# A new order list for all engines, and a maximum of routing codes in three steps instead of one reduction

## The chip, the cores and the metric

The kernel runs on one core of a Trainium2 chip. The core has five engines that run their instruction lists side by side and meet at semaphores: TensorE (PE; its weight loads are shown as PEld), VectorE (DVE), ScalarE (ACT), GpSimdE (POOL) and SyncE (SP), which issues all transfers here. The metric is the device time of one execution, in microseconds, as a median of several runs.

## The reference

Two branches share a layer norm of x (2048 tokens, 576 values); their sum is added to x.

```python
xn = layernorm(x)                                  # S = 2048, D = 576
y_A = irfft2(rfft2(xn) * (w_r + 1j * w_i))         # over tokens and values
q = einsum("nd,dhc->nhc", xn, w_q)                 # 32 heads, 2 x 128
s1 = einsum("nhd,ed->nhe", q[..., :128], k1)       # 8 keys
s2 = einsum("nhd,ed->nhe", q[..., 128:], k2)
e = argmax(s1) * 8 + argmax(s2)                    # one expert of 64 per head
act = gelu(einsum("nd,nhd->nh", xn, u[e]))
y_B = einsum("nh,nhd->nd", act, v[e])              # softmax over one choice is 1
out = x + y_A + y_B
```

## The kernel before

All data stays on the chip after one load of x (`XN`). The program is written in stages, each a function that names its instructions; a planner collects them as operations and issues them in an order of its own.

Branch A goes through matrix products. For each of 16 groups `t` of 128 tokens, `ln` computes mean and spread, and `folds` folds a row of 576 values at its middle: `e`, two halves of 289 (in the trace `t<-XN`, since its slots are called `t1`), then `F`, four quarters (`A<-t` in the trace, slots `A2`). `Rs` is the Fourier matrix of 128 points scaled by the row's spread. `dft128` multiplies (`Rs,A` and `Rs,yl` on TensorE), and each result is split into a rounded part, copied out, and a residual, subtracted by VectorE (`AB<-banks`, `ABL<-banks`). For 16 groups `g` of frequencies follow `d_fwd` (transform along the values, `c,AB` and `c,ABL`), `s_fwd` (the rest of the token transform, 64 x 64 tiles, two groups packed), `s_mul` (the product with the filter `Wt`, two VectorE operations `t<-banks,wx,Wt` a group, combined on GpSimdE as `y` and split as `yh`), and `s_inv` (64-row tiles, `s,yh` and `s,yl`). At the end, per token group, `d_inv` goes back along the values and `fin` adds both branches and writes out.

Branch B never forms the queries. `fold_part` multiplies the differences of the keys (`KP`) into the query weights (32 tiles `w` of 576 KB, five buffers, 32-column tiles of TensorE). Four sums come out; ScalarE copies each to `MT`, VectorE centres it with `mm_`, it is transposed and split into `MU` and `MUL`. `scores` multiplies x transposed (`xT`, made from `xf` by `x_t`) with them, for 256 tokens a round, in eight rounds: 448 score differences a token, 64 choices (`m`) of 7 (`e`), and 64 dot products with `u`. The maximum over the seven is `mx`; `eq` marks where it is reached (0 or 1, two bytes); `eq` times a code per choice (`wt`) goes into the second part of `wk` (slots `w`, so `w<-banks,mx` and `w<-w,wt` in the trace). `route` takes the maximum over the seven codes (`MT<-w`, 128x128 from 896), zeroes it where the first key wins (`MT<-mx,MT`), and forms a table of 8 x 32 codes; `combine` turns it into weights, which `fin` multiplies with `v`.

What sets the order: an operation that may run on more than one engine is written with `FG`, `FV`, `FP` or `FA`, and the letter of `PICK` at its place decides (v VectorE, a ScalarE, g GpSimdE). The list `RANK` has a number per operation. `_Plan.forward` walks time from modelled costs: at each step the engine that is free first takes, among the operations that are ready, the one with the lowest rank, within limits on how many PSUM tiles of a kind are open (`LIMIT`). The order found so is issued; each engine executes its part strictly in that order, SyncE its transfers too. PSUM banks are chosen at the same time.

Of the kernel before, what the change touches and what calls it, by code (L numbers as in the profile page):

```python
# [32 lines left out]
def _consts():  # L33
# [300 lines left out]
class _Plan:  # L334
# [113 lines left out]
    def forward(self, prio):  # L448
# [24 lines left out]
        def choice(e):  # L473

            now, soon, cand = free[e], INF, []
            for i in wait[e]:
                if pre[i]:
                    continue
# [801 lines left out]
```

## Time and profile before

| | |
|---|---|
| median of 3 runs | 226.01 us (225.72 to 227.08) |
| the profiled execution | 225.55 us |
| its span, first to last instruction | 223.8 us |
| busy: TensorE / VectorE / GpSimdE / ScalarE | 195.3 / 198.6 / 152.5 / 128.1 us |
| loaded and written | 38.33 MB, 4.72 MB |
| granted TensorE clock | 1.00 throughout |

A busy time is the time in which an engine has an instruction running. Almost every instruction carries the line number L585, where the planner issues it, so the rows are told apart by the names of their output and inputs (`out<-in`) and by their shapes. A busy TensorE is not one at its peak, since its products overlap in the pipe. [...]

### The profile page before, as it was taken

What the parts mean: (1) busy time and instruction counts of PE and PEld (TensorE: products, weight loads), DVE (VectorE), ACT (ScalarE), POOL (GpSimd) and SP (SyncE); (2) the same over time, 40 slices, a digit from 0 to 9 for tenths busy, and PEclk for the clock granted to TensorE, in tenths of its full rate; (3) what the DMA queues carried; (4) which work ended last, traced back from release to release, by engine and by line L of the source; (5) the groups of instructions that cost most, each with busy time, mean ns of one, the idle gap of its engine ahead of it and who ended that gap; (6) DMA issues with size and microseconds to landing.
All of it is one profiled execution on the core that took longest, in us unless ns stands there. A gap on an engine that the chain in (4) does not pass through costs nothing.

```text
span 223.8 us, 5983 instructions
## 1 busy us (share of the span) xinstructions
PE 195.3 (87%) x2287; PEld 135.7 (61%) x2287; DVE 198.6 (89%) x442; ACT 128.1 (57%) x270; POOL 152.5 (68%) x222
## 2 busy tenths in 40 slices
PE   0069788999999899699899899999979989999993
PEld 0068456677767666565455545655565678787872
DVE  2999999788978997883899999999999999999973
ACT  2278976777767974948475566391545342243330
POOL 3999899991079953745564865893677376689590
PEclk9999999999999999999999999999999999999999
DMA  6999999999999994333525331201100001432415
GB/s 209 421 418 410 364 347 372 408 404 350 343 397 409 400 406 156 113 90 106 151 98 155 89 113 38 61 2 37 35 3 0 3 1 56 160 127 87 158 53 211
DMA packets 14571, 43.41 MB, mean 194 GB/s; under 512 B 1872, under 2 KB 4688, under 8 KB 14160
## 3 DMA queue, kind: packets, MB, share of 16 engines
q1 hardware_dynamic: 14544, 43.05, 52.4%
q8 instruction: 17, 0.28, 0.5%
q14 instruction: 10, 0.08, 0.1%
HBM read 38.33 MB, written 4.72 MB: 192 GB/s over the span
## 4 chain that ended last, share of the span: by engine, by line
PE 41%; DVE 30%; POOL 10%; ACT 6%; issue 6%; DMA 6%; POOLq 0%; ACTq 0%; DVEq 0%
PE banks L585 41%; DVE t L585 7%; DVE w L585 4%; DVE MT L585 4%; DVE AB L585 4%; POOL y L585 3%; DVE A L585 3%; DMA xf<-in_xT_dram 2%; DVE st L585 2%; POOL xT L585 2%; DMA XN<-in_x_dram 2%; DMA w<-in_wq_dram 2%; POOL t L585 1%; DVE ABL L585 1%; POOL A L585 1%
## 5 line engine op out<-in xcount | busy, mean ns | idle before, releaser
L585 PE MATMUL banks<-MU,xT 128*128 128x512 f16 x192 | 46.2, 379 | 0.9 <-DVE w L585 0.7
L585 POOL TENSOR_TENSOR A<-t 128x145 f32<-128x145 f32 (+3 forms) x54 | 36.3, 690 | 5.1 <-DVE t L585 2.8
L585 POOL TENSOR_TENSOR xT<-xf,xT 64x128 f16<-64x128 f32 (+1 forms) x31 | 25.4, 820 | 20.8 <-ACT xT L585 19.4
L585 PEld LDWEIGHTS <-xT 128*128 128x128 f16 x224 | 21.0, 98 | 23.1 <-issue 1.4
L585 PE MATMUL banks<-c,AB 128*128 128x145 f16 (+1 forms) x384 | 34.7, 228 | 0.1
L585 PEld LDWEIGHTS <-AB 128*128 128x128 f16 x384 | 31.5, 122 | 4.6 <-issue 2.9
L585 POOL TENSOR_TENSOR y<-t,t 128x289 f32<-128x289 f32 x30 | 23.0, 788 | 11.2 <-DVE t L585 10.7
L585 POOL TENSOR_TENSOR yh<-y,yh 128x578 f16<-128x578 f32 x16 | 20.4, 1285 | 6.8 <-ACT yh L585 5.7
L585 PE MATMUL banks<-Rs,yl 128*99 128x128 f32 x64 | 11.1, 313 | 15.8 <-DVE Rs L585 13.3
L585 DVE SCALAR_TENSOR_TENSOR t<-banks,wx,Wt 128x578 f32<-128x578 f32 x32 | 24.2, 810 | 0.6 <-issue 0.3
L585 POOL TENSOR_TENSOR t<-XN 128x289 f32<-128x289 f32 x28 | 21.8, 792 | 3.3 <-DMA XN<-in_x_dram 2.9
L585 ACT ACTIVATE yh<-banks,sc 128x580 f32<-128x580 f32 x16 | 11.9, 747 | 20.9 <-PE banks L585 13.5
L585 DVE TENSOR_TENSOR AB<-banks,AB 128x512 f16<-128x512 f32 x32 | 21.6, 677 | 0.9 <-ACT AB L585 0.8
L585 PE MATMUL banks<-A,c 128*128 128x288 f32 x64 | 21.4, 416 | 0.2 <-POOL A L585 0.2
L585 PEld LDWEIGHTS banks<-Rs,yl 128*99 128x99 f32 x64 | 8.6, 187 | 20.4 <-ACT Rs L585 15.6
L585 PE MATMUL banks<-w,KP 128*32 128x288 f32 x256 | 20.9, 416 | 0.0
L585 ACT ACTIVATE AB<-banks 128x512 f16<-128x512 f32 x29 | 16.9, 589 | 6.6 <-PE banks L585 6.5
L585 PE MATMUL banks<-c,ABL 99*128 99x289 f16 (+1 forms) x64 | 18.6, 291 | 2.0 <-DVE t L585 1.6
L585 PE MATMUL banks<-Rs,A 128*128 128x128 f32 x128 | 18.4, 297 | 0.0
L585 DVE TENSOR_REDUCE MT<-w 128x128 bf16<-128x896 bf16 (+1 forms) x16 | 18.2, 1143 | 0.1
L585 PEld LDWEIGHTS banks<-Rs,A 128*128 128x128 f32 x128 | 17.0, 210 | 1.4 <-DVE A L585 0.5
L585 ACT ACTIVATE xf<-xf,bx 128x640 f32<-128x640 f32 x15 | 12.3, 823 | 8.0 <-DMA xf<-in_xT_dram 8.0
(141 smaller groups left out, 431.7 us busy)
## 6 DMA issues: line engine op xcount, KB each, us to landing
w<-in_wq_dram SPq DMA_DIRECT2D x32, 576.0 KB, 6.6
xf<-in_xT_dram SPq DMA_DIRECT2D x16, 320.0 KB, 4.4
Wt<-in_W_dram SPq DMA_DIRECT2D x8, 578.0 KB, 5.9
out_dram<-XN SPq DMA_DIRECT2D x14, 288.0 KB, 2.1
XN<-in_x_dram SPq DMA_DIRECT2D x3, 1154.0 KB, 9.1
s<-in_s_dram SPq DMA_DIRECT2D x16, 192.0 KB, 4.0
XN<-in_x_dram SPq DMA_DIRECT2D x2, 577.0 KB, 4.6
c<-in_c_dram SPq DMA_DIRECT2D x1, 868.5 KB, 8.2
```

The lines of the kernel that those rows point to most:

```text
L585: fn(*[x.place() if isinstance(x, _Ps) else x for x in args], **{k: x.place() if isinstance(x, _Ps) else x for k, x in kw.items()})
```

## The change

It has three parts. First, `RANK` becomes the order itself: operations are sorted by it, and a function `follow` replaces `forward` and only works out start times and PSUM banks along that list; `prepare` and `LIMIT` go. The list is a new one. `PICK` is new, too, and the four small `KP` differences get a letter. The model's cost of a GpSimdE operation with a reversed input is changed, which alters nothing but modelled times and, through them, which PSUM bank a tile gets. Second, the marks and codes of a round lie choice-major (`e` ahead of `m`), so that the comparison reads the scores in PSUM in steps of seven values. Third, the maximum over seven codes is taken in three tensor-tensor steps.

```diff
-        eq = wk[:, 0:896].rearrange("p (t m e) -> p t m e", t=2, e=7)
-        V.tensor_tensor(eq, sv, mx.unsqueeze(3).to_broadcast([128, 2, 64, 7]), op=OP.is_equal)
+        eq = wk[:, 0:896].rearrange("p (t e m) -> p t e m", t=2, e=7)
+        V.tensor_tensor(eq, sv.rearrange("p t m e -> p t e m"), mx.unsqueeze(2).to_broadcast([128, 2, 7, 64]),
+                        op=OP.is_equal)
...
-        wv = wk[:, 896:1792].rearrange("p (m e) -> p m e", e=7)
+        wv = wk[:, 896:1792].rearrange("p (t n) -> p t n", t=2)
...
-        V.tensor_reduce(v0, wv, axis=AX, op=OP.max)
+        V.tensor_tensor(wv[:, :, 192:384], wv[:, :, 0:192], wv[:, :, 192:384], op=OP.max)
+        V.tensor_tensor(wv[:, :, 320:448], wv[:, :, 192:320], wv[:, :, 320:448], op=OP.max)
+        V.tensor_tensor(v0.rearrange("p (t m) -> p t m", t=2), wv[:, :, 320:384], wv[:, :, 384:448], op=OP.max)
...
-    V.tensor_copy(wt.rearrange("p (m e) -> p m e", e=7), mk[:, 20:27].unsqueeze(1).to_broadcast([128, 64, 7]))
+    V.tensor_copy(wt.rearrange("p (e m) -> p e m", e=7), mk[:, 20:27].unsqueeze(2).to_broadcast([128, 7, 64]))
...
-        G.tensor_tensor(KP[:, :, s, 8 * s:8 * s + 7], kT[:, :, 1:8],
-                        kT[:, :, 0:1].to_broadcast([128, 2, 7]), op=OP.subtract)
+        FG.tt(KP[:, :, s, 8 * s:8 * s + 7], kT[:, :, 1:8], kT[:, :, 0:1].to_broadcast([128, 2, 7]), OP.subtract)
...
 RANK = (
-    48, 77, 55, 80, 93, 89, 58, 63, 129, 70, 96, 118, 150, 100, 154, 40, 236, 73, 102, 111, 108, 44, 194,
...
+    3, 19, 14, 16, 76, 107, 2, 75, 51, 39, 143, 181, 0, 6, 15, 22, 13, 25, 1, 12, 40, 237, 5, 4, 8, 9, 7,
...
-        _, order, slot, start = self.forward([-r for r in RANK])
+        order = sorted(range(len(ops)), key=lambda i: RANK[i])
+        _, slot, start = self.follow(order)
```

Three places of the new order follow. On SyncE's queue, around the last tiles of query weights (`w<-in_wq`; `Wt` are filter tiles, `xf` tiles of x transposed, `s` matrices of the token transform), there stood before:

```order
L585 DMA s_0_114<-in_s_dram 128x768
L585 DMA s_1_115<-in_s_dram 128x768
L585 DMA w_118<-in_wq_dram 128x1152
L585 DMA w_122<-in_wq_dram 128x1152
L585 DMA w_119<-in_wq_dram 128x1152
L585 DMA xf_125<-in_xT_dram 128x640
L585 DMA s_3_117<-in_s_dram 128x768
L585 DMA xf_123<-in_xT_dram 128x640
```

and now, at the last tiles of query weights:

```order
L493 DMA s_0_114<-in_s_dram 128x768
L493 DMA w_118<-in_wq_dram 128x1152
L493 DMA w_119<-in_wq_dram 128x1152
L493 DMA w_122<-in_wq_dram 128x1152
L493 DMA s_2_116<-in_s_dram 128x768
L493 DMA s_3_117<-in_s_dram 128x768
L493 DMA Wt_112<-in_W_dram 128x1156
L493 DMA xf_124<-in_xT_dram 128x640
L493 DMA xf_123<-in_xT_dram 128x640
```

Ahead of the last query tile the queue now holds three filter tiles and four `xf` tiles, before five and six; in the whole queue the numbers are the same.

On ScalarE, at the copy of the last folded sum (`MT,mm__94<-banks`), before:

```order
L585 ACTIVATE ABL<-banks 99x2x128
L585 ACTIVATE xf_123<-xf_123,bx 128x640
L585 ACTIVATE xf_125<-xf_125,bx 128x640
L585 ACTIVATE MT,mm__94<-banks 128x576
L585 ACTIVATE A_1_99<-banks 128x578
```

and now:

```order
L493 ACTIVATE AB<-banks 128x4x128
L493 ACTIVATE ABL<-banks 99x2x128
L493 ACTIVATE xT_93<-xf_123 128x640
L493 ACTIVATE MT,mm__94<-banks 128x576
L493 ACTIVATE A_1_99<-banks 128x578
```

The two scalings of freshly loaded `xf` tiles are no longer right ahead of the copy.

On VectorE, in the second round of scores (`mx_131`; `w_121` holds its marks and codes), before:

```order
L585 TENSOR_REDUCE mx_131<-banks 128x128
L585 TENSOR_TENSOR xT_93<-xf_123,xT_93 128x512
L585 TENSOR_TENSOR w_121<-banks,mx_131 128x896
L585 TENSOR_TENSOR AB<-banks,AB 128x4x128
L585 TENSOR_TENSOR ABL<-banks,ABL 33x2x128
L585 TENSOR_TENSOR w_121<-w_121,wt 128x896
L585 TENSOR_TENSOR MT<-MT,fm 128x128
L585 TENSOR_REDUCE MT<-w_121 128x128
```

and now:

```order
L493 TENSOR_REDUCE mx_131<-banks 128x128
L493 TENSOR_TENSOR w_121<-banks,mx_131 128x896
L493 TENSOR_TENSOR w_121<-w_121,wt 128x896
L493 SCALAR_TENSOR_TENSOR t_0_96<-banks,wx,Wt_113 128x578
L493 SCALAR_TENSOR_TENSOR t_1_107<-banks,wx,Wt_113 128x578
L493 TENSOR_TENSOR w_121<-w_121 128x2x192
L493 TENSOR_TENSOR w_121<-w_121 128x2x128
L493 TENSOR_TENSOR y_134<-t_1_107,t_0_96 128x289
L493 SCALAR_TENSOR_TENSOR t_1_97<-banks,wx,Wt_113 128x578
L493 SCALAR_TENSOR_TENSOR t_0_106<-banks,wx,Wt_113 128x578
L493 TENSOR_TENSOR A_0_98<-banks,A_0_98 128x578
L493 TENSOR_TENSOR ABL<-banks,ABL 33x2x128
```

The one reduction has become three tensor-tensor maxima (the third stands two rows further on), with filter products in between.

More of the change, by code (lines that the diff above doesn't have):

```diff
@@ L138 @@
 RANK = (
[66 rows of a table removed]
[66 rows of a table added]
 )
 PICK = (
[L207 to L211 removed]
+    "ggggvgggvagggvvaaavgggaaaagvvvaaaagggvaaaavvvgaaaavgvgvaaavgggaaaagvggaaaagvggaaaagvggaaaaggvgaaaavv"
+    "ggaaaagvvvaaaagvggagaavgggagaaaaaggaaaavgavaaggaaggaaggaaggaavgaagggaaaaggagaggagaaaggagaaaavgaaggaa"
+    "ggaggagagaaaggagaaaaggaaggaaggagaagagaaaggagaaaaggaavgaagvaggagavaaagvagaaaaggaavgaaggagaagagaaaggag"
+    "aaaaggaaggaaggagaavavaaaggagaaaaggagaagggaaaggagaaaggagaggvaaaaaagaagvgagvvagvgagggagvgagggagggagvva"
+    "gvgagggagggagggaggvagggagggaggg"
 )
[L213 removed]
 WORDS = {"mxr": 1, "mxd": 4, "st": 48, "Rs": 128, "t1": 578, "t2": 578, "A2": 578, "y": 578,
@@ L261 @@
 class _Op:
-    __slots__ = ("shape", "tiles", "eng", "calls", "cost", "lat", "deps", "succ", "stage", "pre", "port",
-                 "held", "opens", "after", "bk", "label", "flex")
+    __slots__ = ("shape", "tiles", "eng", "calls", "cost", "lat", "deps", "stage", "port", "bk", "flex")
 def _mask(ap):
@@ L362, in cost @@
             if m == "tensor_tensor":
-                return (60 + 2.05 * n if size_of(out.dtype) == 4 else 175 + 1.92 * n), 75.0
+                rev = any(d[0] < 0 for i in ins for d in i.ap[1:])
+                return (60 + 2.05 * n + (110 if n == 289 and rev else 42 * rev) if size_of(out.dtype) == 4
+                        else 175 + 1.92 * n + (80 if n == 128 else 0)), 75.0
             return ((45 if n > 16 else 280) + (3.02 if ptr else 1.15) * n if ins else 60 + 1.15 * n), 75.0
@@ L399, in add @@
             op.flex = None
-            op.eng, op.calls, op.cost, op.lat, op.deps, op.succ, op.stage = eng, [], c, lat, set(), [], self.stage
+            op.eng, op.calls, op.cost, op.lat, op.deps, op.stage = eng, [], c, lat, set(), self.stage
             op.tiles, op.port, op.bk = tiles, port, []
@@ L430, in latency @@
         return o.lat + (80.0 if o.eng == "vector" and s.eng == "gpsimd" else 0.0)
-    def prepare(self):
-        ops = self.ops
-        for i, o in enumerate(ops):
-            o.pre = set()
-            for j in o.deps:
-                ops[j].succ.append(i)
-        after = [0] * len(ops)
-        for i in reversed(range(len(ops))):
-            for k in ops[i].succ:
-                after[i] |= after[k] | 1 << k
-        for v in {v for o in ops for v in o.tiles if v.kind != "f"}:
-            i = min(v.users)
-            ops[i].pre |= {j for u in v.users for j in ops[u].deps
-                           if j != i and not after[i] >> j & 1 and ops[j].eng != "sync"}
@@ L448, in forward @@
-    def forward(self, prio):
-        ops = self.ops
-        free = {e.name: 0.0 for e in self.engines}
-        need = [len(o.deps) for o in ops]
-        ready = [0.0] * len(ops)
-        pre = [len(o.pre) for o in ops]
-        left = {v: len(v.users) for v in self.tiles}
-        end, slot = dict.fromkeys(left, 0.0), {}
-        wait = {e: [i for i, o in enumerate(ops) if o.eng == e and not o.deps] for e in free}
-        free_at = [0.0] * 8
-        def banks(tiles):
-            f, when, first = list(free_at), 0.0, []
-            for v in tiles:
-                n = v.banks
-                t = {k: max(f[k:k + n]) for k in range(0, 9 - n, n)}
-                lo = min(t.values())
-                k = max((k for k in t if t[k] == lo), key=lambda k: (f[k ^ 1] if n == 1 else -k))
-                f[k:k + n] = [INF] * n
-                when = max(when, lo)
-                first.append(k)
-            return when, first
[L473 to L478, printed above, removed]
-                o, t = ops[i], ready[i]
-                for b in o.bk:
-                    for x, u in seen.get(b, ()):
-                        if x != e and u > t:
-                            t = u
-                if o.opens:
-                    new = [v for v in o.opens if v not in slot]
-                    if new:
-                        k = new[0].kind
-                        tb = banks(new)[0]
-                        if used[k] + len(new) > LIMIT[k] or tb == INF:
-                            continue
-                        t = max(t, tb)
-                soon = min(soon, t)
-                cand.append((t, i))
-            if not cand:
-                return None
-            t0 = max(now, soon)
-            return t0, e, max((prio[i], -i) for t, i in cand if t <= t0)
-        used, port, cold, seen = {k: 0 for k in LIMIT}, 0.0, 4500.0, {}
-        order, start = [], [0.0] * len(ops)
-        shape = None
-        best, stale, full = dict.fromkeys(free), set(free), [0.0, 0.0]
-        while len(order) < len(ops):
-            for e in best:
-                if e in stale:
-                    best[e] = choice(e)
-            t0, e, (_, i) = min((b for b in best.values() if b), key=lambda b: b[0])
-            i = -i
-            wait[e].remove(i)
-            o, cost = ops[i], ops[i].cost
@@ new lines, in follow @@
+    def follow(self, order):
+        ops, free = self.ops, {e.name: 0.0 for e in self.engines}
+        end, late, seen, slot, cur = {}, {}, {}, {}, [None] * 8
+        port, cold, shape, full = 0.0, 4500.0, None, [0.0, 0.0]
+        start = [0.0] * len(ops)
+        for i in order:
+            o, e, cost = ops[i], ops[i].eng, ops[i].cost
+            t = free[e]
+            for j in o.deps:
+                t = max(t, end[j] + self.latency(ops[j], o) + late.get(j, 0.0))
+            for b in o.bk:
+                for x, u in seen.get(b, ()):
+                    if x != e:
+                        t = max(t, u)
+            new = [v for v in sorted(o.tiles, key=lambda v: v.order) if v not in slot] if e == "tensor" else []
+            if new:
+                f = [max(end.get(j, INF) + ops[j].lat for j in v.users) if v else 0.0 for v in cur]
+                for v in new:
+                    n = v.banks
+                    w = {k: max(f[k:k + n]) for k in range(0, 9 - n, n)}
+                    lo = min(w.values())
+                    k = max((k for k in w if w[k] == lo), key=lambda k: (f[k ^ 1] if n == 1 else -k))
+                    slot[v] = k
+                    f[k:k + n], cur[k:k + n] = [INF] * n, [v] * n
+                    t = max(t, lo)
@@ L511, in forward @@
             if e == "tensor":
                 if shape is not None and o.shape[0] != shape:
-                    t0 = max(t0, free[e] + CHANGE)
+                    t = max(t, free[e] + CHANGE)
                 shape = o.shape[1]
-                gap = t0 - free[e]
+                gap = t - free[e]
                 if gap > 2000:
-                    cold = t0 + 3600
-                elif t0 < cold and gap > 600:
+                    cold = t + 3600
+                elif t < cold and gap > 600:
@@ L520, in forward @@
                     cold += gap
-                if t0 < cold:
-                    cost += min(cost, (cold - t0) / 2)
-            elif o.port and port > t0:
-                t0 = port
-            order.append(i)
-            start[i] = t0
-            stale = {e}
-            for k in o.held:
-                pre[k] -= 1
-                if not pre[k]:
-                    stale.add(ops[k].eng)
-            free[e] = t0 + cost
+                if t < cold:
+                    cost += min(cost, (cold - t) / 2)
+            elif o.port:
+                t = max(t, port)
@@ L533, in forward @@
+            start[i], free[e], end[i] = t, t + cost, t + cost
             if o.port:
@@ L536, in forward @@
                 seen.setdefault(b, []).append((e, free[e] + o.lat))
-                stale |= {"vector", "scalar"}
-            if o.opens:
-                new = [v for v in o.opens if v not in slot]
-                for v, k in zip(new, banks(new)[1]):
-                    slot[v] = k
-                    free_at[k:k + v.banks] = [INF] * v.banks
-                    used[v.kind] += 1
-                stale.add("tensor")
-            for v in o.tiles:
-                left[v] -= 1
-                end[v] = max(end[v], free[e] + o.lat)
-                if not left[v]:
-                    free_at[slot[v]:slot[v] + v.banks] = [end[v]] * v.banks
-                    used[v.kind] -= 1
-                    stale.add("tensor")
-            lag = 0.0
             if e == "sync":
-                if t0 > full[1]:
-                    full[0] = t0
+                if t > full[1]:
+                    full[0] = t
                 full[1] = free[e] + 300
-                lag = 2600.0 if t0 - full[0] > 1500 else 0.0
-            for k, lat in o.after:
-                ready[k] = max(ready[k], free[e] + lat + lag)
-                need[k] -= 1
-                if not need[k]:
-                    wait[ops[k].eng].append(k)
-                    stale.add(ops[k].eng)
-        return max(free.values()), order, slot, start
+                late[i] = 2600.0 if t - full[0] > 1500 else 0.0
+        return max(free.values()), slot, start
     def issue(self):
-        self.prepare()
         ops = self.ops
-        self.tiles = sorted({v for o in ops for v in o.tiles}, key=lambda v: v.order)
-        for o in ops:
-            o.held = []
-            o.opens = sorted(o.tiles, key=lambda v: v.order) if o.eng == "tensor" else []
-            o.after = [(k, self.latency(o, ops[k])) for k in o.succ]
-        for i, o in enumerate(ops):
-            for j in o.pre:
-                ops[j].held.append(i)
-        _, order, slot, start = self.forward([-r for r in RANK])
+        order = sorted(range(len(ops)), key=lambda i: RANK[i])
+        _, slot, start = self.follow(order)
         self.order = [(start[i], i) for i in order]
```

6 lines of the change are left out of this document (removed), and 130 rows, old and new, of the table RANK.

## Prediction

> **What bounds the kernel now.** I read the busy times of the page first, then the busy time per stage, cutting the span at VectorE's first and last maximum over scores (`mx`), then single instructions.
>
> ```profile
> PE 195.3 (87%) x2287; PEld 135.7 (61%) x2287; DVE 198.6 (89%) x442; ACT 128.1 (57%) x270; POOL 152.5 (68%) x222
> L585 DVE TENSOR_REDUCE mx<-banks x8: 1074/1076/1092, 104.4 to 178.6; 128x128 f32<-128x896 f32 x8
> 0.00:104.40 104.40, 84.75 (x1069) 60.72 (x1070) 86.49 (x224) 73.11 (x163) 72.95 (x122) 1.00 0.87 328
> 104.40:178.60 74.20, 69.83 (x871) 41.97 (x870) 72.73 (x140) 40.61 (x84) 48.86 (x59) 1.00 0.20 59
> 178.60:223.80 45.20, 40.71 (x351) 33.01 (x349) 39.37 (x80) 14.35 (x24) 30.73 (x43) 1.00 0.28 106
> 0.00:89.90 89.90, 71.80 (x916) 52.36 (x916) 76.36 (x201) 62.41 (x145) 65.68 (x113) 1.00 0.95 362
> 177.20:220.30 43.10, 41.99 (x362) 34.14 (x362) 40.25 (x82) 14.66 (x25) 31.71 (x43) 1.00 0.26 99
> ```
>
> Columns after the stretch and its length: busy us of PE, PEld, DVE, ACT, POOL, then clock, DMA share, GB/s. Three stages have three limits. Before 104.4 us VectorE is busy 86.5 us and idle 17.9, of which 13.5 lie before 89.9 (89.9 - 76.4). In the middle it is busy 72.7 of 74.2 us: the limit, with TensorE (69.8) close behind. At the end TensorE is busy 42.0 of 43.1 us.
>
> The first stage hangs on memory and on a chain behind it:
>
> ```profile
> 0.73 3.89 DMA XN<-in_x_dram
> 50.00:60.00 10.00, 9.79 (x106) 7.72 (x106) 8.78 (x30) 7.39 (x18) 1.06 (x3) 1.00 0.98 350
> 70.00:80.00 10.00, 9.43 (x159) 6.07 (x156) 9.85 (x21) 8.69 (x18) 9.24 (x11) 1.00 1.03 404
> 78.95 0.33 SPq L585 DMA_DIRECT2D w<-in_wq_dram  x1
> 87.29 0.69 PE L585 MATMUL banks<-w,KP 128*32 128x288 f32 x8
> 87.56 1.55 ACT L585 ACTIVATE xf<-xf,bx 128x640 f32<-128x640 f32 x2 [3.13 <-DMA xf<-in_xT_dram]
> 89.01 0.63 ACT L585 ACTIVATE MT<-banks 128x576 f32<-128x576 f32 x1
> 89.77 0.15 DVE L585 TENSOR_SCALAR mm__94<-mm__94 128x1 f32<-128x1 f32 x1 [0.91 <-ACT MT L585]
> 93.67 0.68 DVE L585 SCALAR_TENSOR_TENSOR MU<-banks,sc,MU 128x448 f16<-128x448 f32 x1 [0.49 <-ACT MU L585]
> ```
>
> The first load ends at 4.6 us. The DMA engines are full (share 1) until 80 us. The last tile of query weights is issued at 78.95, its fold ends on TensorE at 88.0; ScalarE copies the sum (`MT`, 89.01), VectorE centres it (89.77) and finishes `MU` (93.67), which every score needs. ScalarE is late by 1.0 us, because two scalings of `xf` stand ahead of the copy and waited for their transfer.
>
> **The change, part by part.** *1. Transfers.* Ahead of the last query tile on SyncE's queue stand four `xT` and three `W` loads, where six and five stood.
>
> ```profile
> w<-in_wq_dram SPq DMA_DIRECT2D x32, 576.0 KB, 6.6
> xf<-in_xT_dram SPq DMA_DIRECT2D x16, 320.0 KB, 4.4
> Wt<-in_W_dram SPq DMA_DIRECT2D x8, 578.0 KB, 5.9
> ```
>
> Two of each are 2 x 320 + 2 x 578 = 1796 KB, or 1.84 MB. At the 404 and 350 GB/s above that is 4.6 to 5.3 us; I say the last tile can land **4.8 us earlier**. With ScalarE's two scalings moved behind the copy, 1.0 us more is open, so 5.8 in all. The query tiles share five buffers and SyncE issues in order, so it also waits for TensorE's folds, which grow no faster by themselves. The two `W` tiles now come behind; their `s_mul` products stand behind the last fold in VectorE's list too. If a tile is not there by then, VectorE waits with all that is queued behind (the scores' maxima), up to one landing of 5.9 us.
>
> *2. Folds of x pass from GpSimdE to VectorE.* Before the first `mx`, the 289-wide folds `t` on VectorE go from 4 to 15, and five `A` sums of 145 come over. It loses three evictions (`CAST AB`) to ScalarE, and two evictions (`AB`, `ABL`, here 0.6 and 0.34) and one 578-wide residual fall behind the first `mx`.
>
> ```profile
> L585 DVE TENSOR_TENSOR t<-XN 128x289 f32<-128x289 f32 x4 | 2.8, 702 | 0.0
> L585 POOL TENSOR_TENSOR t<-XN 128x289 f32<-128x289 f32 x28 | 21.8, 792 | 3.3 <-DMA XN<-in_x_dram 2.9
> L585 DVE TENSOR_TENSOR A<-t 128x288 f32<-128x288 f32 x5 | 2.6, 518 | 0.4 <-POOL t L585 0.4
> L585 DVE CAST AB<-banks 128x512 f16<-128x512 f32 x3 | 2.0, 673 | 0.0
> L585 DVE TENSOR_TENSOR AB<-banks,AB x32: 664/676/692, 19.7 to 177.0; 128x512 f16<-128x512 f32 x32
> L585 DVE TENSOR_TENSOR ABL<-banks,ABL 33x256 f16<-33x256 f32 x32 | 12.9, 404 | 1.0 <-ACT ABL L585 1.0
> L585 DVE TENSOR_TENSOR A<-banks,A 128x578 f16<-128x578 f32 x16 | 11.9, 750 | 4.0 <-ACT A L585 4.0
> ```
>
> An instruction's own time is its row less about 0.07 us, by which the next one starts early. So 11 x 0.63 = 6.9; five of 145 at an estimated 0.28 (a little over half of the 288 row) = 1.4; less 3 x 0.6 = 1.8; less 0.6 + 0.34 + 0.7 for what falls behind; less some 0.7 in smaller moves. VectorE does **4.2 us more** before the first `mx`, and GpSimdE some 11 us less. The cover is VectorE's idle time: of the 13.5 us before 89.9, 4.6 are the first load, 8.9 remain, and 4.7 are left after the new work. So the bounds of this stage are 5.8 us earlier (memory and ScalarE alone) and 4.2 later (no idle time can be used). VectorE's row is the nearer one, since it must be there when the last tile is folded: I take half of the 4.7, **2.4 us earlier**.
>
> *3. The maximum of the routing codes.* A reduction over 896 two-byte values goes; three tensor-tensor maxima of 384, 256 and 128 values come, eight times.
>
> ```profile
> L585 DVE TENSOR_REDUCE MT<-w x16: 1066/1144/1220, 108.8 to 206.9; 128x128 bf16<-128x896 bf16 x8, 128x32 f32<-128x1024 bf16 x8
> L585 DVE TENSOR_TENSOR w<-w,MT x16: 397/412/651, 111.8 to 204.9; 128x512 bf16<-128x512 bf16 x16
> L585 DVE TENSOR_TENSOR w<-banks,mx x8: 1068/1078/1092, 106.8 to 181.4; 128x896 bf16<-128x896 f32 x8
> L585 DVE TENSOR_TENSOR w<-w,wt x8: 605/694/1076, 108.0 to 183.2; 128x896 bf16<-128x896 bf16 x8
> 118.68 1.08 DVE L585 TENSOR_TENSOR w<-w,wt 128x896 bf16<-128x896 bf16 x1
> 117.61 1.66 POOL L585 TENSOR_TENSOR xT<-xf,xT 64x128 f16<-64x128 f32 x2 [1.33 <-ACT xT L585]
> ```
>
> The two-byte products price it where nothing holds them: 605 ns for 896 and 397 for 512, so 0.54 ns an element above 120. That makes 327, 258 and 189 ns; each less 70, together 0.56 us, against 1.00 for the reduction: 0.44 saved a round. But the same products reach 1076 and 651, and the longest ran beside two GpSimdE instructions that read SBUF. The reduction has no such spread. So each new maximum waits between 0 and 0.47 us (1076 - 605), 0 to 11 us over 24. The medians lie 0.09 and 0.02 above the least, the long ones raise the means further; I take 0.09 each, near the median, so 0.27 a round, and **0.17 us saved a round**.
>
> [...]
>
> In the middle stage six rounds change: 1.0 us less. A 512-wide `xT` residual (1.5 us in that stage) goes, three of 64 x 128 (an estimated 0.3 each) come, the evictions and the residual of part 2 add 1.6, smaller moves take 0.9. From 72.7 that leaves 71.8: **0.9 us earlier**.
>
> *4. The comparison* (`eq`, row `w<-banks,mx`) now reads PSUM in steps of seven values. I cost that at nothing, since its 1078 ns equal those of the reduction over as many values. No row shows such steps; it may stay, or double to about 2.1 (rival C).
>
> *5. TensorE's order.* A change of tile shape costs time:
>
> ```profile
> 136.77 1.47 PE L585 MATMUL banks<-MU,xT 128*128 128x512 f16 x6
> 138.50 0.28 PE L585 MATMUL banks<-id,MT 128*128 128x128 f16 x2
> 146.97 1.89 PE L585 MATMUL banks<-MU,xT 128*128 128x512 f16 x8
> 148.80 0.40 PE L585 MATMUL banks<-s,yh 64*128 64x128 f16 x8
> ```
>
> Eight score products (six and two `MUL`) before a full-size one take 1.73 us, eight before one of 64 rows 1.83: 0.1 a change. The new list has 70 changes for 88; 14 of the 18 are gone before the first score, where they are inside the 2.4, four in the middle, where VectorE ends last: 0.
>
> *6. The last stage* has the same products, no change of shape in either list, and 0.5 us more of VectorE's work beside 5.8 idle: 0. The planning that goes ran on the host, at no time here.
>
> The sum is -2.4 - 0.9 = -3.3. Against the profiled execution's own 225.55 (span 223.8 and 1.75 around it) that is 222.25. The median of the runs, 226.01, lies 0.46 above that execution; half of it is added: **222.5 us**.
>
> **The rivals.** *A: memory's whole gain.* VectorE packs its front so well that 4.8 us arrive, and 1.5 in the middle: 225.8 - 6.3 = 219.5. For it speaks the DMA share of 1; against it VectorE's 4.7 us of cover, which it would have to use up. *B: no gain.* The 4.2 us of folds hold the first `mx` where it is, and blocked maxima eat what they save: 225.8. For it: the blocked rows, and more work for an engine that is 89% busy. *C: the stepped reading, slower.* If a comparison takes twice its 1.0 us, six in the middle add 6.0, where only 1.5 are idle and none waits to be used: 222.5 + 6.0 = 228.5. It decides from 0.55 us a comparison on (3.3 / 6). Against it: the `AB` row spreads only from 664 to 692, though half of its 32 read and write SBUF in runs of four values and half in runs of 64 or more. [...] *D: the last stage stalls.* Five inverse transforms stand ahead of the first output, and all sixteen 288-wide subtractions are GpSimdE's; if TensorE waits for it in three of the sixteen steps, about 2 us each in a stage that has 1.1 idle, it is 222.5 + 6 - 1 = 227.5.
>
> **How the numbers follow.** About 1% is what a measurement of this kernel can tell from no change. Forecast 0.37 (221 to 224.2, three quarters of it below 223.75), A 0.19, B 0.27, C 0.11, D 0.06. Faster: 0.28 + 0.19 = 0.47. Same: 0.09 + 0.27 = 0.36. Slower: C and D, 0.17. The range reaches from 219, just past A, to 228.3, past D and short of C; it leaves out most of C and some of A.
>
> **What would show it.** The last query tile issued near 74 us; `MT` copied right behind the fold; the first `mx` near 102; 73 us from first to last `mx`; 45 behind. The three maxima near 0.33, 0.26 and 0.19 us, with long ones among them, and `eq` at 1.08. I am wrong if the first `mx` comes after 105 though the tile landed early (the folds), if the last stage exceeds 46, or if `eq` is above 1.6.

## The result, and the profile after

The changed kernel takes **214.14 us** (median of 4 runs, 213.50 to 214.62), where before took 226.16 (4 runs on the same chip): a ratio of 0.946, 95% interval 0.942 to 0.950. The prediction said 222.5, with a range of 219.0 to 228.3, so the time lies 4.9 us below its lower end. The profiled execution took 214.62 us, span 212.8: 11.0 less than before's 223.8. Executions more than 1.5% above the fastest of the same kernel are left out of all ratios.

The busy times of the page, and then the three stages, cut as in the prediction at the first and the last maximum over scores:

```profile
PE 192.7 (91%) x2287; PEld 134.7 (63%) x2287; DVE 195.5 (92%) x471; ACT 129.8 (61%) x280; POOL 136.1 (64%) x199
0.00:96.70 96.70, 80.94 (x1025) 58.39 (x1027) 85.33 (x233) 70.01 (x161) 62.24 (x102) 1.00 0.88 328
96.70:167.00 70.30, 70.19 (x921) 43.05 (x916) 69.39 (x154) 45.84 (x96) 43.85 (x54) 1.00 0.30 99
167.00:212.80 45.80, 41.56 (x353) 33.23 (x351) 40.81 (x87) 13.93 (x24) 30.04 (x45) 0.99 0.28 104
L493 DVE TENSOR_REDUCE mx<-banks x8: 1071/1080/1093, 96.7 to 167.0; 128x128 f32<-128x896 f32 x8
L493 DVE TENSOR_TENSOR w<-banks,mx x8: 1069/1078/1093, 97.8 to 168.7; 128x896 bf16<-128x896 f32 x8
```

The first stage is 7.7 us shorter (104.4 to 96.7), the middle 3.9 (74.2 to 70.3), the end 0.6 longer. In the first stage VectorE is busy 85.33 us, 1.2 less than before, not 4.2 more; in the middle 69.39 against 72.73. `eq` has not moved from 1.08 us.

The chain of the front, in order of time (start, duration):

```profile
76.40 0.81 SPq L493 DMA_DIRECT2D w<-in_wq_dram  x2
84.26 0.65 ACT L493 ACTIVATE MT<-banks 128x576 f32<-128x576 f32 x1 [3.25 <-PE banks L493]
89.54 0.68 DVE L493 SCALAR_TENSOR_TENSOR MU<-banks,sc,MU 128x448 f16<-128x448 f32 x1
90.35 0.82 PE L493 MATMUL banks<-MU,xT 128*128 128x512 f16 x3
96.67 1.09 DVE L493 TENSOR_REDUCE mx<-banks 128x128 f32<-128x896 f32 x1 [0.92 <-PE banks L493]
```

The last query tiles are issued at 76.4 and 76.8, the last one 2.2 us earlier than before's 78.95; the sum is copied at 84.26 instead of 89.01, right behind the fold; `MU` comes at 89.54 instead of 93.67. So **4.1 us** lie ahead of `MU`, and they have three sources. The last tile's way from issue to landing and what TensorE did around it and around `MU`, first before, then after:

```profile
DMA to landing us min/median/max: 6.5/6.5/6.5
86.44 0.55 PE L585 MATMUL banks<-c,AB 128*128 128x145 f16 x6
94.38 1.68 PE L585 MATMUL banks<-A,s 64*64 64x289 f16 x48
97.02 2.75 PE L585 MATMUL banks<-MU,xT 128*128 128x512 f16 x12
...
76.78 6.19 DMA w<-in_wq_dram
83.02 1.18 PE L493 MATMUL banks<-w,KP 128*32 128x288 f32 x16 [0.21 <-DMA w<-in_wq_dram]
```

In before the last tile landed at 85.4 (78.95 + 6.5), but its fold started only at 87.29, 1.9 us later, behind forward transforms (`c,AB`). Now it lands at 83.0 and TensorE waits for it. The landing thus came 2.4 us earlier, and the fold's end 3.8 (88.0 to 84.2): the 1.4 between them are TensorE's order. The last 0.3 are ScalarE's: the copy is no longer 1.0 us late, but most of that is lost again on the way to `MU`.

The other **3.6** lie behind `MU`: TensorE goes to the scores at once (90.35), where before it did forward transforms first, from 94.38 to 97.02, and 1.0 us of them between the two halves of the first round.

VectorE's groups by shape (busy us, mean ns of one), those of before first:

```profile
L585 DVE SCALAR_TENSOR_TENSOR A<-t,rr 128x145 f32<-128x145 f32 x16 | 8.9, 561 | 2.0 <-POOL t L585 1.5 <-POOL rr L585 0.5
L585 DVE TENSOR_SCALAR MT<-MT 128x16 int32<-128x16 f32 x16 | 3.8, 261 | 0.0
L585 DVE SCALAR_TENSOR_TENSOR MT<-MT,sc,act 128x128 f32<-128x128 int32 x8 | 3.9, 483 | 0.0
L585 DVE TENSOR_TENSOR t<-XN x4: 459/750/850, 5.0 to 25.0; 128x289 f32<-128x289 f32 x4
...
L493 DVE TENSOR_TENSOR t<-XN 128x289 f32<-128x289 f32 x15 | 6.6, 443 | 0.0
L493 DVE SCALAR_TENSOR_TENSOR A<-t,rr 128x145 f32<-128x145 f32 x16 | 6.7, 431 | 0.7 <-POOL rr L493 0.4 <-POOL t L493 0.3
L493 DVE TENSOR_SCALAR MT<-MT 128x16 int32<-128x16 f32 x16 | 3.3, 211 | 0.0
L493 DVE SCALAR_TENSOR_TENSOR MT<-MT,sc,act 128x128 f32<-128x128 int32 x8 | 3.2, 403 | 0.0
L493 DVE TENSOR_TENSOR w<-w 128x384 bf16<-128x384 bf16 x8 | 2.8, 346 | 0.0
L493 DVE TENSOR_TENSOR w<-w 128x256 bf16<-128x256 bf16 x8 | 2.4, 300 | 0.1
L493 DVE TENSOR_TENSOR MT<-w 128x128 bf16<-128x128 bf16 x8 | 1.7, 213 | 0.0
```

A fold `t` takes 443 ns on average, where the four of before took 702. One of those four took 459 (the fourth line is least, median and most); each of the other three ended 0.3 us behind the end of a GpSimdE instruction that ran beside it. Rows that the change does not touch are shorter too: `A<-t,rr` by 130 ns each, the small steps on the codes (`MT<-MT`) by 50 to 80.

### The profile page after: what moved, and what is told of

Read it like the earlier page. It is cut to its first block, busy times and chain, and to the rows that moved or that the text cites. A ratio compares the mean times of both kernels' runs of the same rounds, so it can differ in the third digit from the quotient of the medians.

```text
span 212.8 us, 5984 instructions
## 1 busy us (share of the span) xinstructions
PE 192.7 (91%) x2287; PEld 134.7 (63%) x2287; DVE 195.5 (92%) x471; ACT 129.8 (61%) x280; POOL 136.1 (64%) x199
## 4 chain that ended last, share of the span: by engine, by line
PE 44%; DVE 30%; DMA 8%; POOL 8%; issue 6%; ACT 1%; SPq 0%; POOLq 0%; DVEq 0%
PE banks L493 44%; DVE t L493 7%; DMA w<-in_wq_dram 6%; DVE w L493 5%; DVE A L493 5%; POOL A L493 4%; DVE MT L493 4%; DVE AB L493 3%; DMA XN<-in_x_dram 3%; POOL t L493 2%; DVE mx L493 2%; DVE st L493 2%; DVE XN L493 1%; DVE ABL L493 1%; POOL mv L493 1%
## 5 line engine op out<-in xcount | busy, mean ns | idle before, releaser
L493 POOL TENSOR_TENSOR A<-t 128x287 f32<-128x287 f32 (+3 forms) x46 | 31.4, 698 | 10.5 <-DVE t L493 5.7
L493 PE MATMUL banks<-Rs,A 128*128 128x128 f32 x128 | 19.8, 302 | 13.9 <-DVE Rs L493 12.6
L493 POOL TENSOR_TENSOR xT<-xf,xT 128x512 f16<-128x512 f32 (+1 forms) x28 | 24.1, 863 | 11.9 <-PE banks L493 5.5
L493 POOL TENSOR_TENSOR y<-t,t 128x289 f32<-128x289 f32 x30 | 20.8, 713 | 16.7 <-DVE t L493 16.1
L493 ACT ACTIVATE AB<-banks 128x512 f16<-128x512 f32 x32 | 18.7, 591 | 3.1 <-PE banks L493 2.9
L493 ACT ACTIVATE ABL<-banks 99x256 f16<-99x256 f32 x32 | 12.0, 381 | 8.4 <-PE banks L493 7.8
L493 POOL TENSOR_TENSOR t<-yh 128x288 f32<-128x288 f32 x16 | 12.2, 765 | 6.6 <-ACT yh L493 4.1
L493 ACT ACTIVATE MT<-banks 128x256 f16<-128x256 f16 (+1 forms) x12 | 5.7, 472 | 16.5 <-PE banks L493 14.7
L493 POOL TENSOR_TENSOR t<-XN 128x289 f32<-128x289 f32 x17 | 13.1, 776 | 3.0 <-DMA XN<-in_x_dram 2.2
L493 DVE SCALAR_TENSOR_TENSOR XN<-banks,sc,XN 128x576 f32<-128x576 f32 (+1 forms) x18 | 13.1, 743 | 1.5 <-PE banks L493 1.4
```

What stands on the lines that cost most here:

```text
L493: fn(*[x.place() if isinstance(x, _Ps) else x for x in args], **{k: x.place() if isinstance(x, _Ps) else x for k, x in kw.items()})
```

## The experiments

Each kernel was timed beside before on its own chip; ratios are to that, with a 95% interval. "The list" is the order of all operations, "letters" are `PICK`.

### The maxima alone, and the list without them

**e1_max_only**: before's list, letters and PSUM banks.

```diff
-        V.tensor_reduce(v0, wv, axis=AX, op=OP.max)
+        V.tensor_tensor(wv[:, :, 192:384], wv[:, :, 0:192], wv[:, :, 192:384], op=OP.max)
+        V.tensor_tensor(wv[:, :, 320:448], wv[:, :, 192:320], wv[:, :, 320:448], op=OP.max)
+        V.tensor_tensor(v0.rearrange("p (t m) -> p t m", t=2), wv[:, :, 320:384], wv[:, :, 384:448], op=OP.max)
```

> The order, the engines and the PSUM banks of before; only the codes choice-major and the three maxima in place of the reduction. Theory 'order' (the new list and letters carry nearly all of the 12 us, the maxima what the prediction gave them, 0.17 us a round): 225 to 226 us, with 73 to 74 us from first to last maximum over scores. Rival 'maxima' (VectorE is the limit of the middle stage, so what the three steps save there, 0.4 to 0.5 us a round, comes out whole and makes up the 3.9 us that the middle stage lost): 222 to 223 us, middle stage 70 to 71.

Measured: 230.62 us, ratio 1.015 (1.009 to 1.022). **Slower** by 1.5%, which neither theory had. The groups, the middle stage, and the worst place on VectorE with what ran on GpSimdE:

```profile
L499 DVE TENSOR_TENSOR w<-w 128x384 bf16<-128x384 bf16 x8 | 3.5, 439 | 0.0
L499 DVE TENSOR_TENSOR w<-w 128x256 bf16<-128x256 bf16 x8 | 3.9, 491 | 0.3
104.50:180.30 75.80, 70.43 (x872) 42.02 (x870) 73.75 (x152) 40.66 (x84) 49.19 (x59) 1.00 0.19 58
150.17 1.78 DVE L499 TENSOR_TENSOR w<-w 128x384 bf16<-128x384 bf16 x2
150.41 1.39 POOL L499 TENSOR_TENSOR yh<-y,yh 128x578 f16<-128x578 f32 x1
```

Two maxima that take 0.65 us in after (346 and 300 ns) took 1.78 and ended at 151.95, 0.15 us after GpSimdE's residual (151.80). In before's list the maxima take 1.15 us a round (each counted to the start of the next instruction, as all sums of this kind below), more than the reduction's 1.00; in the new list 0.70. So in before's list the swap loses. Whether GpSimdE's instructions held the maxima up these rows do not show, only that they ran at the same time. Of the 2.8 us by which the profiled execution is longer than before's, 1.6 lie in the middle and 1.1 in the end; why the end is longer is open.

**e2_reduction_back**: after, with the reduction over the old layout at the third maximum's place. **g1_reduction_first**: the same, the reduction at the first maximum's place in seven rounds of eight.

```diff
-        V.tensor_tensor(wv[:, :, 192:384], wv[:, :, 0:192], wv[:, :, 192:384], op=OP.max)
...
+        V.tensor_reduce(v0, wv, axis=AX, op=OP.max)
```

> The list, letters and banks of after; the one reduction over the old layout stands where the third maximum stood. Theory 'order': 215 to 215.5 us (0.17 us a round lost). Rival 'maxima': 217.5 to 218.5 us, all of it in the middle stage, whose length returns to 73 to 74 us.

> As e2_reduction_back, but in seven of eight rounds the reduction stands where the first of the three maxima stood. If e2_reduction_back lost its 6 us because the reduction stood too late in VectorE's list (its place): 215 to 217 us. If it lost them because the list leaves no room for 0.3 us more of VectorE a round without TensorE waiting (the list fits its own operations only): 218.5 to 221.5 us again, with VectorE's work 3 to 4.5 us above after's 195.5.

Measured: 220.86 (0.972, 0.965 to 0.978) and 219.09 (0.967, 0.960 to 0.973). So in the new list the maxima are worth about 5 us (g1), and the place of the reduction is not the reason. (Of what e2 lost beyond that, 2.3 us lie in its front, where this edit changes nothing and one tile came late; see h2 below.) g1's middle:

```profile
96.30:170.50 74.20, 71.68 (x923) 43.70 (x920) 73.38 (x141) 46.05 (x96) 43.98 (x54) 1.00 0.28 94
```

Its front is 96.3 us, after's 96.7; its middle is before's 74.2 again, VectorE's work there 4.0 us above after's. Six rounds of maxima explain 1.8 of that (6 x 0.30); the rest are other VectorE instructions that took longer, above all `w<-w,MT` (0.9), `w<-w,wt` (0.8) and the steps on `MT` (0.8). What lengthened them is not shown here. The list and the maxima are one thing: neither gains in the middle without the other.

### Half a list at a time

**e3_front_new**: the new list and letters up to the first `mx`, then what is left in before's order. **e4_rest_new**: the reverse. Both with the maxima. **g2_rest_letters_old**: after's list, but 33 letters behind the first `mx` are before's.

```diff
 e3: -list behind mx: new       +list behind mx: before's rest, before's letters
 e4: -list ahead of mx: new     +list ahead of mx: before's, before's letters
 g2: -letters behind mx: new    +letters behind mx: before's; the list stays
```

> The new list and letters up to the first maximum over scores, then what is left in before's order with before's letters; three maxima. Theory 'each stage keeps its own gain': front 97, middle 73 to 74, so 218 to 219 us. Rival 'the front only hands work on' (the forward transforms that no longer stand ahead of the first scores, 3.8 us of TensorE's time, are done later instead): front 97, middle 76 to 78, so 221 to 223 us.

> Before's order and letters up to the first maximum over scores, then what is left in the new order with the new letters; three maxima. Theory 'each stage keeps its own gain': front 104, middle 70 to 71, so 221 to 223 us. Rival 'the front only hands work on': the middle, with 3.8 us of TensorE's work already done, takes 67 to 68, so 218 to 220 us.

> After's list, transfers, banks and maxima, but 33 letters of the work behind the first maximum over scores are before's again (evictions AB, y sums, small copies, the folds of the output). Theory 'letters and list belong together': the middle 72 to 75 and the tail 46 to 48, 217 to 221 us. Rival 'the list alone': 214 to 215.5 us. Rival 'letters were chosen for VectorE's relief': VectorE's busy time rises by 2 us or more and the middle with it, 216 to 217 us.

Measured: 230.44 (1.016, 1.010 to 1.023), 222.45 (0.980, 0.973 to 0.986), 222.84 (0.977, 0.967 to 0.986). e4's stages keep what each list gives alone:

```profile
0.00:104.30 104.30, 84.28 (x1069) 60.28 (x1070) 86.84 (x224) 72.79 (x163) 73.16 (x122) 1.00 0.87 328
104.30:173.90 69.60, 68.26 (x870) 41.02 (x869) 67.98 (x151) 41.88 (x89) 42.59 (x51) 1.00 0.20 63
```

So the rest of the new list with the maxima is worth 4.6 us in the middle behind the old front (74.2 to 69.6), and what e4 lacks is the front's 7.6. e3 keeps after's front (96.5), but is no clean test of the rest: at the seam TensorE waited 4.8 us for a scaling on ScalarE, and then it ran slowly:

```profile
96.50:181.70 85.20, 75.41 (x923) 45.19 (x918) 77.31 (x156) 44.69 (x91) 50.87 (x61) 0.96 0.25 81
103.38 0.37 PE L493 MATMUL banks<-c,wm 128*1 128x128 f32 x1 [4.79 <-ACT t L493]
103.55 3.62 PE L493 MATMUL banks<-MU,xT 128*128 128x512 f16 x8
98.60:108.00 9.40, 4.62 (x25) 2.49 (x27) 3.37 (x6) 5.43 (x10) 2.91 (x4) 0.66 0.55 196
```

Eight score products take 3.62 us there, at a mean clock of 0.66, where before's eight took 1.89. The two make 6.5 us of the 9.4 by which e3's middle (85.2) exceeds e1's (75.8); whether the rest is work that the front only hands on, e3 leaves open, and h1 below asks it again. In g2 the middle is 75.8 us, with VectorE's work at 74.2, 5.5 and 4.8 us above after's: letters chosen for one list are wrong for another. (2.1 us more of g2's loss lie in its front, whose letters are after's: the late tile again.)

### The front: folds, letters, ScalarE

**f1_folds_back**: after, 21 operations of the front (13 folds `t` and 8 sums `A`) from VectorE back to GpSimdE. **f3_front_engines_new**: e4 with the front's new letters on before's front list. **f4_scalings_behind**: e4 with this one exchange on ScalarE:

```diff
-ACTIVATE xf_123<-xf_123,bx 128x640
-ACTIVATE xf_125<-xf_125,bx 128x640
 ACTIVATE MT,mm__94<-banks 128x576
+ACTIVATE xf_123<-xf_123,bx 128x640
+ACTIVATE xf_125<-xf_125,bx 128x640
```

> After's list and transfers, but 21 instructions of the front (15 folds t of x, 289 wide, among them, and six sums A) go back from VectorE to GpSimdE, at their places in the list. Theory of the prediction (these folds cost VectorE 4 to 7 us that GpSimdE does for nothing): the first maximum over scores at 92 to 97 us, 210 to 215 us in all. [...]

> Before's list up to the first maximum over scores, with the new letters (folds on VectorE, evictions on ScalarE); behind it the new list and letters; three maxima. Against e4_rest_new (222.5 us on its chip, front 104.3 us), which differs by the front's letters alone. Theory 'engines' (the letters carry the front's 7.7 us): front 96 to 98, 214 to 216 us. Rival 'order' (letters chosen for another list fit no better): front 103 to 107, 221 to 226 us.

> As e4_rest_new, but ScalarE's two scalings of xf stand behind the copy of the last folded sum. Theory of the prediction (ScalarE is 1.0 us late there, and the chain to the scores hangs on it): first maximum at 103.3, 221.5 us. Rival 'TensorE has other work between': front stays at 104, 222 to 223 us.

Measured: f1 0.970 (0.959 to 0.981), its profiled execution 217.91 us; f3 227.26 (1.002, 0.998 to 1.006); f4 223.45 (0.988, 0.983 to 0.994). f1's front, its `A<-t,rr`, and what TensorE waited for between 12 and 55 us (total, times, longest):

```profile
0.00:100.20 100.20, 81.13 (x1023) 58.69 (x1025) 85.56 (x211) 70.40 (x161) 73.03 (x123) 1.00 0.86 317
L493 DVE SCALAR_TENSOR_TENSOR A<-t,rr 128x145 f32<-128x145 f32 x16 | 9.3, 593 | 4.1 <-POOL t L493 3.8 <-POOL rr L493 0.3
PE banks L493 <- ACT Rs L493: 1.5, 1, 1.5
PE banks L493 <- DVE rr L493: 1.4, 1, 1.4
```

With 21 instructions less VectorE is as busy as after's (85.56 against 85.33): with GpSimdE busy 73.03 us instead of 62.24, VectorE's other rows take longer, `A<-t,rr` 593 ns each instead of 431. The folds come late and the front is 3.5 us longer. The folds cost VectorE nothing on balance. On before's list the same letters give a front of 110.2 us (f3): they are no gain by themselves. f4 was expected to bring 1.0 us; its first `mx` came at 106.6, 2.3 us later than e4's. The centring came 0.5 us earlier on TensorE (90.31 for 90.8), but the next steps waited instead, and three waits close together were followed by a lower clock, so f4 does not isolate ScalarE's 1.0 us:

```profile
PE banks L493 <- DVE mxr L493: 1.5, 1, 1.5
PE banks L493 <- DVE mm__94 L493: 0.8, 1, 0.8
PE banks L493 <- ACT t L493: 0.4, 1, 0.4
95.73 2.62 PE L493 MATMUL banks<-A,s 64*64 64x289 f16 x48
93.00:99.00 6.00, 5.67 (x98) 4.39 (x99) 3.87 (x11) 2.53 (x7) 2.61 (x3) 0.72 0.27 70
```

### The transfers

**f2_loads_ahead**: after, four loads in front of the last three query tiles on SyncE. **g4_loads_ahead_but_one**: the same without the last of them.

```diff
+DMA xf_124<-in_xT_dram 128x640
+DMA xf_125<-in_xT_dram 128x640
+DMA Wt_112<-in_W_dram 128x1156
+DMA Wt_113<-in_W_dram 128x1156      (f2 only)
 DMA w_118<-in_wq_dram 128x1152
 DMA w_119<-in_wq_dram 128x1152
 DMA w_122<-in_wq_dram 128x1152
```

> After's list, but two xT loads and two W loads stand on SyncE's queue ahead of the last three tiles of query weights again. Theory of the prediction (memory sets the last fold; 1.84 MB is 4.6 to 5.3 us): last query tile issued 4 to 5 us later, first maximum at 100 to 102, 218 to 220 us. Rival 'the queue waits for buffers, not for bytes' (the issue moved 2.2 us only): first maximum at 97 to 99, 214 to 216.5 us.

> As f2_loads_ahead, but the W load whose buffer came free at 81 us only stays behind the last query tiles; two xT loads and one W load (1.25 MB, 3.0 to 3.6 us at 404 to 350 GB/s) stand ahead of them. Theory of bytes: last query tile issued 3 us later than after's 76.8, first maximum at 99.5 to 100.5, 217 to 218.5 us. Theory 'the queue waits for a buffer' (f2_loads_ahead lost its 8 us to the one wait): first maximum at 96.5 to 98.5, 214 to 216 us.

Measured: f2 222.75 (0.986, 0.979 to 0.993), g4 218.08 (0.961, 0.953 to 0.968). f2's queue, what SyncE and TensorE waited for, and TensorE's wait in g4:

```profile
73.15 8.13 SPq L493 DMA_DIRECT2D Wt<-in_W_dram  x2
81.38 1.52 SPq L493 DMA_DIRECT2D w<-in_wq_dram  x3
SPq L493 <- DVE MUL L493: 7.4, 1, 7.4
PE banks L493 <- DMA w<-in_wq_dram: 6.1, 1, 6.1
82.42 0.69 PE L493 MATMUL banks<-w,KP 128*32 128x288 f32 x8 [2.02 <-DMA w<-in_wq_dram]
```

The fourth load's buffer was in use until 81 us (`MUL` is made from what lies in it), and SyncE waited for it 7.4 us with three query tiles behind. g4 takes that wait away: its last query tile is issued at 77.1, as after's 76.8, but TensorE waits 2.0 us for query tiles (0.9 in after), and the front is 100.6 us long, 3.9 more than after's. So both theories hold in part. 1.25 MB ahead do not delay the issue, but the landing: 2.0 us of waiting, and with the slower products behind it (the mean clock from 82 to 90 us was 0.79) 3.9 in all, where 3.0 to 3.6 were expected of the bytes alone. The buffer's wait, with the lower clock behind it (0.63 from 81 to 90 us), is the other 4.1 (104.7 less 100.6).

### Scores first: a gain, or a handover?

**h1_scores_later**: after, two inverse transforms (2.0 us) moved ahead of the first round of scores.

```diff
+TensorE: MATMUL banks<-s,yh / banks<-s,yl, two groups
 TensorE: MATMUL banks<-MU,xT / banks<-MUL,xT, first round
-TensorE: MATMUL banks<-s,yh / banks<-s,yl, two groups
```

> After, with the two inverse transforms (2.0 us of TensorE's time) that stand right behind the first round of scores moved ahead of it; nothing else changes. Theory 'scores first is a gain, since VectorE is busy from the first maximum on': first maximum 2 us later at 98.5 to 99, 215.5 to 216.5 us. Rival 'handover': first maximum at 98.5 to 99, the middle 2 us shorter, 213.5 to 214.7 us, as after.

Measured: 219.01 (0.963, 0.958 to 0.968), while after on that chip was at 0.945 (h4 below). First `mx` at 100.7, and the middle:

```profile
100.70:171.00 70.30, 68.37 (x847) 40.79 (x846) 69.40 (x154) 45.52 (x95) 42.01 (x52) 1.00 0.25 84
```

TensorE has 1.8 us less to do in the middle than after's 70.19, and the middle is not a tenth of a microsecond shorter. It is 70.30 in after, f1, f2, g3, g4, h1, h2 and h3, with the first `mx` anywhere from 95.9 to 104.7: VectorE's work of 69.4 sets it. So what the first `mx` gains, the end gains, and scores first is a gain. (Of the 4.0 us by which `mx` moved, 2.0 are the moved work; TensorE also waited for its inputs, 1.7 us for the longest. h1 moved inverse transforms; that before's forward ones count alike follows from the unchanged middle, but was not run.)

### A better version?

**g3_head**: after, `kT` behind the first two loads of x, and the first two `Rs` earlier on VectorE. **h2_w_ahead**: after, the filter tile `Wt_112` ahead of two `s` tiles on SyncE. **h3_x_ahead**: h2, and the last load of x two places earlier. **h4_after_again**: after, on h2's and h3's chip.

```diff
 h2: +DMA Wt_112<-in_W_dram 128x1156
      DMA s_2_116<-in_s_dram 128x768
      DMA s_3_117<-in_s_dram 128x768
     -DMA Wt_112<-in_W_dram 128x1156
 h3: +DMA XN<-in_x_dram 128x2308
      DMA w_120<-in_wq_dram 128x1152
      DMA w_121<-in_wq_dram 128x1152
     -DMA XN<-in_x_dram 128x2308
```

> After, with the load of kT behind the first two loads of x on SyncE, and the first two scaled matrices Rs (which the first matmul waits for, 12.6 us) made on VectorE as soon as rr is there. If the front hangs on TensorE's start: first matmul at 11, first maximum over scores at 95 to 95.7, 212.5 to 213.5 us. If it hangs on the transfers and their buffers: first matmul at 11, the rest unchanged, 213.5 to 215 us.

> After, with the last filter tile W of the front ahead of two s tiles on SyncE (some 0.9 us earlier); ScalarE reads it at 86 us, and in several runs TensorE waited 0.9 to 2.0 us for that. If the wait is what spreads the runs: 213.3 to 214.0 us and a smaller spread than after's. If not: after's time.

> As h2_w_ahead, and the last load of x two places earlier on SyncE, ahead of two tiles of query weights, since TensorE waits 1.5 us for rr of those rows at 31.8 us. If that wait is on the path: 212.5 to 213.5 us. If the front hangs on the query tiles, which then land later: 214 to 216 us.

> After unchanged, as the measure of the other three on the same chip: 213.5 to 214.7 us.

Measured: g3 217.28 (0.959, 0.953 to 0.965), h2 214.44 (0.943, 0.938 to 0.948), h3 214.22 (0.941, 0.937 to 0.946), h4 215.57 (0.945, 0.940 to 0.951). g3 lost 3 us, which neither theory had: VectorE began earlier, but GpSimdE's differences of the late `kT` stand ahead of its folds, the first matmul came at 12.67 instead of 12.59, and more waits followed. h3 has the shortest front, `mx` at 95.9, and its six runs lie between 213.5 and 214.5; that it beats after is possible, but the intervals overlap. The reason for h2 is a tile that after needs just in time. In e2, where it came late, the same place reads (then the same 48 products in after, and the same wait in h4):

```profile
88.02 0.27 PE L498 MATMUL banks<-c,wm 128*1 128x128 f32 x1 [1.71 <-ACT t L498]
89.62 3.11 PE L498 MATMUL banks<-A,s 64*64 64x289 f16 x48
88.74 1.68 PE L493 MATMUL banks<-A,s 64*64 64x289 f16 x48
89.15 0.27 PE L493 MATMUL banks<-c,wm 128*1 128x128 f32 x1 [2.00 <-ACT t L493]
```

A scaling of the tile on ScalarE comes 1.7 us late, and the products behind it take 3.11 us instead of 1.68. It happens to after itself: h4 missed its 213.5 to 214.7, and its profiled execution (218.37 us) waits 2.0 us there and has its first `mx` at 100.1, with nothing changed. So 2 or 3 us of front in a single profile can be this tile and not the edit; in f1, f2, g4 and h1 the other waits shown say that it is the edit. h2 and h3 do not wait there; h2's runs spread over 1.7 us, h4's over 3.9.

## Why the prediction was wrong, point by point

**What bounds the kernel: right for the middle and the end.** VectorE sets the middle (70.30 us in eight kernels), TensorE the end. The front hangs on the query tiles and on the chain to `MU`, as said, but also on what TensorE does ahead of each.

**The step that failed: TensorE's order, put at nothing.** Part 5 looked at the new order for changes of shape only, and part 1 took the last fold to end when its tile allows. In before that fold started 1.9 us behind its tile's landing, and the scores stood behind forward transforms. The new order saves 1.4 us ahead of `MU` and 3.6 behind it, 5.0 of the front's 7.7. The 1.4 are read from the rows, no run changes them alone; that time ahead of the scores counts in full, h1 shows.

**1. Transfers: mis-sized.** Up to 4.8 us were named; the tile landed 2.4 earlier. It was issued at 76.8, not near 74: SyncE waited for buffers that TensorE frees (15.1 us in all between 60 and 80 us), which the prediction names and does not price. Of ScalarE's 1.0 us, 0.3 arrived at `MU`. That bytes ahead of the tiles do count, g4 shows: 1.25 MB, two thirds of those reckoned with, made TensorE wait 2.0 us instead of 0.9.

**2. Folds: mis-sized, and VectorE's sum got the wrong sign.** "11 x 0.63" came from the mean of four folds, 702 ns, of which three ended 0.3 us behind a GpSimdE instruction; the least, 459, is near what a fold takes in the new list, 443. Less 0.07 for the overlap, fifteen take 5.5 us where four took 2.5, so 3.0 more, not 6.9. And in the new list, where GpSimdE does less (62.24 us of the front for 72.95), other rows are shorter: `A<-t,rr` lost 2.2 us, the small `rr<-rr` steps 1.5. VectorE's front changed by -1.2, not +4.2. With this term the prediction halved the cover and with it the gain; that its 2.4 is just what the landing gained is chance. f1 bears the term's failure out: with the folds on GpSimdE VectorE is no less busy and the front 3.5 us longer.

**3. The maxima: mis-sized, and wrongly taken by themselves.** 0.56 us a round at the pace of the least rows and 0.27 of waiting made 0.83; measured are 0.70 in the new list and 1.15 in the old one. The saving is 0.30 a round instead of 0.17, 0.8 us more over six rounds. The larger part of the middle's error is the other work: the prediction counted how much longer the new maxima may be beside GpSimdE and not that a new list can make other rows shorter. In the middle the small code steps `MT<-MT` and `MT<-MT,sc,act` alone lost 2.5 us, 0.4 of it because one round's last steps fall behind the cut. VectorE's work fell by 3.3, not 0.9, and the stage by 3.9. What exactly shortens these rows stays open, and so does what lengthens those that the prediction calls blocked (`w<-w,wt`, 605 to 1076 ns): the rows show what ran beside them, not what held them.

**4. and 6. The comparison and the end: right.** `eq` in steps of seven values takes 1078 ns, as before, so rival C falls; the end is 45.8 us, 0.6 more than forecast, so D falls too. **5.** TensorE's busy time fell by 2.6 us; 18 changes fewer at 0.1 would give 1.8 of it, an estimate that no run here tests.

Of the rivals A came nearest in time (219.5), but not by its mechanism: memory brought 2.4 of its 4.8 us, and TensorE's order, which no rival names, brought more. Of the signs, `MT` right behind the fold, the three maxima (346, 300 and 213 ns), `eq` and the end came as named; the issue of the last tile, the first `mx` (96.7 for 102) and the middle (70.3 for 73) did not.

## What to carry to other kernels

Read a new order as work that moves, not only as a list of costs: ask what each engine does between the moment an input is there and the moment it is used. Price an instruction from the shortest rows of its kind (459 ns for the fold, where the mean of four was 702 and the new list's 443), and look for untouched operations whose rows may get shorter: the distance between their least and their mean is an estimate of the gain that is to be had (`A<-t,rr`: least 356 ns and mean 561 before, mean 431 after). In a list made for one set of operations, do not judge an operation by putting it in or taking it out alone; the same three maxima cost 3.9 us in one list and were worth about 5 in the other. Where one engine sets a long stage, its first instruction of that stage is the due date: here, what brought it forward counted in full, and what was done earlier elsewhere did not (1.8 us less for TensorE in h1, and the middle still 70.30).

## What the runs showed of the hardware

The comparison of 896 fp32 values on VectorE reads PSUM in steps of seven values as fast as in order: its median is 1078 ns before (in order) and after (in steps).

TensorE's granted clock fell behind some idle stretches, also short ones: behind a wait of 1.7 us (e2) 48 products took 3.11 us instead of 1.68, at a mean clock of 0.76 from 86 to 93 us; behind one of 4.8 us (e3) eight scores took 3.62 instead of 1.89, at 0.66. Yet in h1, with a wait of 1.7 us between 85 and 105 us, the mean clock is 1.00 both ahead of 100.7 us and behind it. What decides between e2 and h1 stays open.
